# A windowed-attention and MLP kernel on one core: three more buffers in spent weights' space, a first copy in halves, last stores on two queues, and a new written-out order

## The chip, the core and the metric

The kernel runs on one core of a Trainium2 chip. TensorE (PE) multiplies, VectorE (DVE), ScalarE (ACT) and GpSimd (POOL) do the rest, and SyncE (SP) issues most of the DMAs. The metric is the device time of one execution in microseconds; the median of three runs stands for the kernel.

## The reference, cut to what matters

```python
x = layernorm(A_x)                                    # 2048 x 512
q, k, v = split(x @ wqkv)                             # 32 heads of 16
logits[s, w] = q[s] . k[s - 2*w] / 4,  w = 0..7       # masked where s - 2*w < 0
s = (softmax(logits) applied to v[s - 2*w]) @ wo
h  = gelu(layernorm(x) @ w1); four channel groups of h moved by -1, +1, -2, +2 positions
x1 = x + moved(h) @ w2
g  = silu(x1 + gelu(layernorm(x1) @ w3) @ w4)         # w3: 512 x 1376
out = x + s * g
```

All tensors are bf16. The mixer uses x normalized once, the MLP normalizes it once more.

## The kernel before, in words

The 2048 rows are worked in 4 chunks of 512, a chunk in 4 tiles of 128 rows. There is no planner at run time and no loop: a string `ORDER` (line 16) lists all steps by hand, and the last lines of the kernel call them one after the other. A token such as `w1.6.4` is step `w1` for tile 6 in PSUM bank 4. Each engine runs its own instructions in the order in which they stand in the list, and waits by semaphore for what another engine must have done; so where a token stands fixes what it queues behind.

The steps that matter here, with their engine and line:

- **Front.** `ldxp` and `ldxc` load x (SP). `st`, `nm0`, `nmv` take statistics and normalize (DVE). For chunk 0 PE transposes the normalized tile (`tr0`, line 353) and ACT copies it out of PSUM into `xnT` (`ev0a`, line 357); later chunks are transposed by DMA (`xT`).
- **Products of x, four matmuls of 512 columns a step.** `v` (line 460), `w1` (485) and `qk` (432) on PE; ACT takes the results away (`ev`, `eh`, `eqk`), `sv` stores v to DRAM from POOL's queue (`vt` has 3 buffers), `hTr` transposes h into `hT` by DMA (504), and `w2` (600) reads `hT`; `xa` (607, DVE) adds its result to x.
- **Attention.** `pw` (DVE, 519) multiplies q with shifted k, eight times a chunk. `lg` (PE, line 532) sums each head: two of the eight at once, 32 matmuls of 128 columns, in weight tiles of 128 x 32. `smx`, `ex`, `sms`, `smn` are the softmax (DVE, ACT) in one `E_c` buffer, and `tE` (587) transposes it into `att` by DMA. `vl` (699) loads shifted rows of v from DRAM as two halves of 512 KB into a value buffer `vs`, `vp` (705, DVE) multiplies them with `att`, and `ws` (718, PE, weight tiles of 128 x 32 again) sums over the window. Each `ws` of a chunk reads all four value buffers of the chunk. `oTr` (737) transposes the result by DMA, `wo` (757) is the last product, `sg` (764) multiplies with the gate.
- **MLP.** `x1Tr` (644) transposes, `w3` (657) and `eg` (666) make 11 pieces of h3 a chunk, `w4` (674) is 11 matmuls a tile, `ya` (681) adds, `si` (685) takes silu.
- **End.** Tiles 0 to 11 are added onto a copy of x in the output by DMAs with addition (`pre`, `soa`). Tiles 12 to 15 are finished on chip: `oTp` and `eoT` transpose on PE and ACT, `wo` for tiles 12 to 14, `woh` (782) in two halves of 256 columns for tile 15, then `ge`, `gb`, `fav` and `sgh`, `favh` (ACT and DVE) and the stores `so` and `soh`.

A rotating buffer is chosen when the program is built. `tags` (129) gives each use the buffer that was used longest ago, and can add buffers from a given use on. The value buffers are four of their own, from use 8 on also the space of `wqk_sb` (weights of `qk`), from use 12 on that of `hT`. `att` is a single buffer. PSUM has six banks for the products and one area of two for `lg`.

The loads of SP's queue are issued in their order; one that waits holds those behind it.

Of the kernel before, what the change touches and what calls it, by code (L numbers as in the profile page):

```python
# [16 lines left out]
ldxp.s.0 c_warm c_small ldv.s.0 kh.0 warmup.10.512.0 sqw ldv.s.1 c_ident ldxp.s.1 ldw1.s.0
c_elog st.0 st.1 sq0.0 nm0.0 sq0.1 rp.0 nm0.1 tr0.0.0 warmup.8.128.1 ev0a.0 tr0.1.2 v.0.0 rs.0
st.2 ev0a.1 ldw1.s.1 ldxp.s.2 st.3 c_sel sq0.2 v.1.2 ldxp.s.3 ev.0 rr.0 ldqk.s.0 nm0.2 sq0.3
ldqk.s.1 ev.1 c_zero nm0.3 tr0.2.0 w1.1.1 rp.1 ev0a.2 ldxc.s.2 ldwo.s.2 st.5 v.2.0 eh.1 st.4  # L20
w1.2.2 rs.1 st.6 tr0.3.3 sv.0 w1.0.4 ev0a.3 st.7 ldw2.s sv.1 ev.2 qk.0.0.3 rr.1 rp.2 eh.2 sv.2
rp.3 qk.0.2.0 eh.0 rs.2 eqk.0.0 v.3.2 hTr.0 rs.3 nmv.4 eqk.0.2 nmv.5 qk.0.7.3 rr.2 nmv.6 xT.2
ev.3 qk.0.6.0 st.11 eqk.0.7 sv.3 st.8 qk.0.5.2 eqk.0.6 rr.3 w1.3.3 nmv.7 eqk.0.5 st.10 qk.0.3.0
ldxc.s.3 eh.3 st.9 xT.3 qk.0.4.2 eqk.0.3 rp.5 rp.4 qk.0.1.3 rs.4 eqk.0.4 vl.s.0.0 kh.1 eqk.0.1
nb.4 vl.s.0.1 w1.4.2 rr.4 nm.9 rs.5 pw.0.0 vl.s.1.0 v.4.3 nm.8 v.5.0 pw.0.2 ev.4 eh.4 vl.s.3.1
w1.5.4 sv.4 pw.0.1 ev.5 xT.4 qk.1.2.2 eh.5 sv.5 pw.0.3 qk.1.5.0 eqk.1.2 rr.5 qk.1.7.4 eqk.1.5
st.15 ldwo.s.3 hTr.1 qk.1.4.2 st.12 eqk.1.7 lg.0.1 nb.5 eqk.1.4 st.13 v.6.4 nm.11 pw.0.6 nm.10
lg.0.0 v.7.2 ev.6 pw.0.7 sv.6 w1.6.4 vl.s.1.1 ev.7 pw.0.4 xT.5 lg.0.3 sv.7 pw.0.5 w1.7.2 hTr.2
v.8.0 st.14 lg.0.2 rp.6 rp.7 eh.7 w2.1.3 rs.7 smx.0 eh.6 ev.8 rs.6 v.9.2 hTr.3 w2.0.0 sv.8 ev.9
w1.9.4 sv.9 vl.s.2.0 nb.6 xa.1 ex.0 vl.s.2.1 qk.2.3.2 rr.7 st3s.1 qk.2.0.3 rr.6 xa.0 qk.2.6.1  # L30
eqk.2.0 nb.7 sms.0 eh.9 w2.4.0 qk.2.1.3 v.11.5 eqk.2.6 xa.4 nm.14 v.10.1 smn.0 nm.15 w2.3.0
ldw3.s.1 ev.10 st3s.0 tE.0 nm.12 w2.2.4 sv.10 xa.3 nm.13 qk.2.2.1 rq.0 xa.2 r3.0 ev.11 qk.2.7.0
st3s.3 eqk.2.2 sv.11 eqk.2.3 st3s.2 qk.2.5.5 vl.s.3.0 eqk.2.7 nm3.0 eqk.2.1 qk.2.4.2 rq.1 nm3.1
eqk.2.5 r3.1 st3s.4 w1.11.3 x1Tr.0 eqk.2.4 nm3.2 w1.8.5 vp.0 eh.11 w1.10.2 eh.8 w2.5.3 hTr.4
eh.10 vp.2 qk.1.6.5 hTr.5 qk.1.3.2 eqk.1.6 qk.1.1.0 kh.2 eqk.1.3 xa.5 vp.3 qk.1.0.5 eqk.1.1
w2.7.3 eqk.1.0 xT.7 w2.6.0 pw.1.3 xT.6 w2.8.5 pw.1.2 w2.9.2 v.14.1 xa.6 xa.7 lg.1.1 ev.14 st3s.6
v.13.3 ldw3.s.0 sv.14 pw.1.7 w1.13.1 pre.s.1 ev.13 pw.1.0 w1.12.0 sv.13 eh.13 w1.14.3 pw.1.1
eh.12 w1.15.1 hTr.6 eh.14 pw.1.4 lg.1.0 eh.15 v.12.3 ldw4.s.0 pw.1.6 hTr.7 ev.12 pw.1.5 qk.3.5.1
qk.3.2.0 sv.12 vp.1 eqk.3.5 kh.3 qk.3.6.3 eqk.3.2 qk.3.7.1 eqk.3.6 w2.11.0 eqk.3.7 pw.2.0 lg.1.2
xa.11 ws.1.1 ws.2.3 pw.2.2 eo.1 ws.0.0 eo.2 ws.3.4 eo.0 pw.2.1 w2.12.1 vl.s.4.1 eo.3 qk.3.1.0  # L40
oTr.1 nm3.3 xa.12 qk.3.4.4 eqk.3.1 xa.8 x1Tr.1 xa.9 qk.3.0.1 eqk.3.4 st3s.8 qk.3.3.2 eqk.3.0
st3s.9 w2.10.4 eqk.3.3 vl.s.8.0 st3s.7 vl.s.6.1 w2.15.1 xa.10 ldw4.s.1 w3.0.2.2 rq.3 rq.4
ldw4.s.2 xa.15 r3.3 vl.s.7.0 pw.3.0 w3.0.3.4 eg.0.2 r3.4 vl.s.6.0 w3.0.0.1 oTr.0 eg.0.3 nm3.7
nm3.6 w3.0.8.2 st3s.5 eg.0.0 x1Tr.3 w3.0.10.4 st3s.10 eg.0.8 st3s.11 w3.0.5.1 eg.0.10 rq.2
w3.0.4.2 st3s.15 r3.2 eg.0.5 rq.5 w3.0.1.4 st3s.12 r3.5 eg.0.4 nm3.5 w3.0.6.1 eg.0.1 nm3.4
lg.1.3 eg.0.6 w3.0.9.4 pw.2.3 pre.s.0 w3.0.7.1 eg.0.9 smx.1 vl.s.8.1 w2.14.2 vl.s.5.1 eg.0.7
x1Tr.2 w2.13.4 w4.0.1 xa.14 ex.1 xa.13 vl.s.7.1 st3s.14 st3s.13 w4.3.4 ya.0 rq.7 sms.1 si.0 r3.7
w4.1.1 ya.3 smn.1 si.3 w4.2.4 ya.1 nm3.10 si.1 nm3.11 ldwo.s.1 nm3.8 x1Tr.5 w3.1.1.1 nm3.9 ya.2
w3.1.3.2 rq.6 pw.2.4 si.2 tE.1 r3.6 eg.1.1 w3.1.9.4 w3.1.0.5 vl.s.5.0 nm3.14 x1Tr.4 w3.1.7.0
nm3.15 eg.1.0 eg.1.9 w3.1.5.1 vp.6 eg.1.7 eg.1.3 w3.1.6.4 eg.1.5 w3.1.8.2 eg.1.6 vp.7 w3.1.2.1  # L50
eg.1.8 w3.1.4.4 eg.1.2 w3.1.10.2 eg.1.4 vp.5 w3.2.0.1 eg.1.10 v.15.4 eg.2.0 nm3.13 vl.s.4.0
w4.5.2 ev.15 nm3.12 x1Tr.6 sv.15 x1Tr.7 w4.4.4 ya.5 si.5 vp.4 w4.7.2 vl.s.12.0 ya.4 si.4 lg.2.0
ya.7 ws.5.4 pw.2.6 si.7 lg.2.1 ws.6.2 eo.5 ws.7.1 pw.3.1 eo.6 w4.6.4 eo.7 pw.2.5 pw.2.7 lg.2.2
ws.4.1 ya.6 lg.2.3 pw.3.3 si.6 w3.2.9.4 eo.4 pw.3.5 w3.2.2.2 eg.2.9 w3.2.4.1 smx.2 w3.2.3.0
eg.2.4 eg.2.2 ldwo.s.0 w3.2.7.4 eg.2.3 pre.s.2 pw.3.2 w3.2.5.2 ex.2 w3.2.1.0 pw.3.4 wo.0.1
vl.s.13.0 eg.2.7 w3.2.6.5 sms.2 lg.3.0 lg.3.1 vl.s.12.1 eg.2.6 lg.3.2 eg.2.5 vl.s.13.1 w3.2.10.4
sg.0 eg.2.1 vl.s.11.0 smn.2 w3.2.8.2 soa.0 eg.2.10 wo.1.0 eg.2.8 pw.3.6 tE.2 wo.2.4 sg.1 oTr.2
w4.8.2 pw.3.7 soa.1 sg.2 soa.2 w4.10.4 ya.8 vl.s.9.1 si.8 vl.s.9.0 vp.8 vl.s.10.0 wo.3.2 wo.5.0
oTr.3 w3.3.0.1 sg.3 vl.s.10.1 sg.5 wo.4.5 soa.3 eg.3.0 ya.10 soa.5 lg.3.3 sg.4 w4.11.4 vl.s.11.1
smx.3 soa.4 si.10 w4.9.1 vp.9 ex.3 wo.6.5 ya.11 sms.3 si.11 w3.3.2.4 w3.3.10.0 eg.3.2 w3.3.5.2  # L60
sg.6 w3.3.8.3 smn.3 soa.6 w3.3.3.5 eg.3.5 eg.3.10 vp.10 w3.3.7.2 eg.3.3 eg.3.8 w3.3.9.0 eg.3.7
w3.3.4.3 vp.11 eg.3.9 w3.3.6.2 eg.3.4 w3.3.1.0 eg.3.6 ya.9 tE.3 ws.8.3 eg.3.1 ws.9.2 si.9
ws.11.0 ws.10.1 w4.12.5 vl.s.14.0 eo.10 eo.11 vp.13 eo.8 vl.s.14.1 eo.9 w4.13.3 vl.s.15.0
vl.s.15.1 ya.12 oTr.4 vp.12 si.12 w4.15.5 ya.13 vp.14 si.13 w4.14.3 ya.15 wo.7.2 vp.15 si.15
wo.8.5 oTr.5 wo.9.0 ya.14 ws.12.1 sg.8 si.14 ws.13.3 ws.14.4 sg.7 eo.12 soa.8 ws.15.5 eo.13 sg.9
soa.7 oTp.12.2 eo.15 wo.11.1 soa.9 eo.14 eoT.12 oTp.13.5 sg.11 wo.10.4 eoT.13 soa.11 oTp.15.1
sg.10 oTp.14.5 eoT.15 wo.13.2 eoT.14 soa.10 wo.12.1 ge.13 wo.14.5 gb.13 ge.12 fav.13 woh.15.0.2
gb.12 so.s.13 ge.14 woh.15.1.1 fav.12 sgh.15.0 so.s.12 gb.14 favh.15.0 sgh.15.1 soh.s.15.0
fav.14 favh.15.1 so.s.14 soh.s.15.1
# [4 lines left out]
def kernel(  # L74
# [280 lines left out]
    @step  # L355
    def ev0a(i):
        nc.scalar.activation(xnT_tile(0)[:, i, :, :], tr_t.pop(i), AF.Copy)
# [502 lines left out]
```

## Time and profile before

| | |
|---|---|
| median of 3 runs | 193.5 us (193.16 to 193.62) |
| the profiled execution's own time | 192.78 us |
| its span, first to last instruction | 191.0 us |
| PE busy | 97% of the span, 1430 matmuls |
| DVE, ACT, POOL busy | 86%, 63%, 22% |
| granted TensorE clock | 1.0 |
| moved by DMA | 39.25 MB, mean 205 GB/s |

The span is what the profile's rows add up to; the execution's own time is 1.8 us longer, and the median of the runs is 0.7 us above the profiled execution. A row of the timeline gives the start, the time taken, engine, line, operation and tiles, and how many instructions it merges. The end of a matmul is modelled and overlaps the next one, so that PE's pace is read from start to start: sixteen matmuls of 512 columns between two starts of the timeline take 3.45 us, four of them 0.86 us.

### The profile page before, as it was taken

How to read it: one execution, taken by the hardware profiler on the slowest of the kernel's cores; microseconds unless marked ns; L12 is line 12 of the kernel's file. 1: busy time of each engine (PE TensorE's matmuls, PEld its weight loads, DVE VectorE, ACT ScalarE, POOL GpSimd, SP SyncE). 2: the span in 40 equal slices, each digit the busy share in tenths (PEclk: the TensorE clock that was granted, in tenths of full speed). 3: DMA queues.
4: the chain of work that ended last, by engine and by line, in shares of the span. 5: the costliest groups of instructions: out<-in, count | busy, mean ns of one | idle time of the engine just before them, and what ended most of it. 6: DMA issues, size and time to landing. Idle time of an engine off the chain costs nothing.

```text
span 191.0 us, 3682 instructions
## 1 busy us (share of the span) xinstructions
PE 184.7 (97%) x1430; PEld 86.2 (45%) x1430; DVE 163.8 (86%) x270; ACT 120.8 (63%) x190; POOL 42.2 (22%) x70
## 2 busy tenths in 40 slices
...
GB/s 185 330 328 281 202 293 282 266 276 263 228 141 116 293 165 128 220 304 324 217 308 137 195 139 137 250 6 317 123 135 239 278 232 27 55 270 224 64 127 114
DMA packets 47841, 39.25 MB, mean 205 GB/s; under 512 B 35250, under 2 KB 41888, under 8 KB 47776
## 3 DMA queue, kind: packets, MB, share of 16 engines
...
q0 software_dynamic: 2528, 3.69, 10.0%
...
## 4 chain that ended last, share of the span: by engine, by line
PE 77%; DMA 12%; DVE 4%; SPq 2%; ACT 2%; issue 1%; DVEq 0%; ACTq 0%
PE mm L657 20%; PE mm L674 15%; PE mm L432 13%; PE mm L600 7%; PE mm L485 6%; PE mm L757 5%; PE mm L460 4%; DMA oT<-o 4%; DMA hT<-ht 4%; PE lg L532 3%; PE mm L718 3%; DMA xc<-in_A_x_dram 2%; DMA att<-E_c 2%; SPq L267 1%; DVE vs L705 1%; DVE st L330 1%
## 5 line engine op out<-in xcount | busy, mean ns | idle before, releaser
L657 PE MATMUL mm<-x1T,w_sb 128*128 128x512 bf16 (+1 forms) x176 | 39.3, 379 | 0.1
L705 DVE TENSOR_TENSOR vs<-vs,att 128x4096 bf16<-128x4096 bf16 x16 | 36.2, 2286 | 3.5 <-DMA att<-E_c 2.5
L674 PE MATMUL mm<-w_sb,h 128*128 128x512 bf16 (+1 forms) x176 | 39.1, 379 | 0.0
L519 DVE TENSOR_TENSOR pw<-qT,kT 128x2048 bf16<-128x2048 bf16 x32 | 37.6, 1219 | 1.4 <-PE lg L532 1.4
L666 ACT ACTIVATE h<-mm 128x512 bf16<-128x512 f32 (+1 forms) x44 | 24.7, 599 | 8.8 <-PE mm L657 8.5
L432 PE MATMUL mm<-xnT,wqk_sb 128*128 128x512 bf16 x128 | 29.3, 379 | 0.0
L674 PEld LDWEIGHTS <-h 128*128 128x128 bf16 (+1 forms) x176 | 16.9, 98 | 21.1 <-issue 0.8
L657 PEld LDWEIGHTS <-w_sb 128*128 128x128 bf16 (+1 forms) x176 | 17.3, 100 | 20.3 <-issue 0.5
L685 ACT ACTIVATE xr<-xr 128x512 bf16<-128x512 bf16 x16 | 10.1, 630 | 24.7 <-DVE xr L681 24.6
L820 POOL DMA_DIRECT2D out_dram<-xr x12 | 10.5, 945 | 58.0 <-DVE xr L764 57.7
L432 PEld LDWEIGHTS <-wqk_sb 128*128 128x128 bf16 x128 | 12.5, 98 | 15.1
...
L460 PE MATMUL mm<-wv_sb,xnT 128*128 128x512 bf16 x64 | 16.0, 380 | 0.0
L600 PE MATMUL mm<-w_sb,hT 128*128 128x512 bf16 x64 | 15.6, 379 | 0.1
L485 PE MATMUL mm<-w_sb,xnT 128*128 128x512 bf16 x64 | 15.6, 379 | 0.0
L681 DVE TENSOR_TENSOR xr<-mm,xr 128x512 bf16<-128x512 f32 x16 | 10.9, 681 | 4.7 <-PE mm L674 4.5
L757 PE MATMUL mm<-wo_sb,oT 128*128 128x512 bf16 x60 | 14.6, 379 | 0.2 <-DMA oT<-o 0.2
L470 ACT ACTIVATE vt<-mm 128x512 bf16<-128x512 f32 x16 | 9.5, 594 | 7.5 <-PE mm L460 6.1
L624 POOL TENSOR_TENSOR rstd<-nmr,mhalf 128x2 f32<-128x2 f32 x8 | 8.0, 998 | 28.0 <-DVE nmr L617 28.0
L496 ACT ACTIVATE ht<-mm,rs 128x512 bf16<-128x512 f32 x16 | 10.8, 688 | 4.9 <-DMA hT<-ht 3.2
L330 DVE BATCH_NORM_STATS2 st<-xc 128x6 f32<-128x512 bf16 x16 | 10.8, 674 | 2.9 <-DMA xc<-in_A_x_dram 2.9
L441 ACT ACTIVATE kT<-mm 128x512 bf16<-128x512 f32 x16 | 9.6, 599 | 4.4 <-PE mm L432 3.4
...
## 6 DMA issues: line engine op xcount, KB each, us to landing
vs<-v_dram SPq DMA_DIRECT2D x32, 512.0 KB, 6.2
v_dram<-vt POOLq DMA_DIRECT2D x16, 128.0 KB, 4.6
out_dram<-in_A_x_dram SPq DMA_DIRECT2D x3, 512.0 KB, 4.8
out_dram<-xr POOLq DMA_DIRECT2D x12, 128.0 KB, 3.9
...
xc<-in_A_x_dram SPq DMA_DIRECT2D x4, 256.0 KB, 4.9
wqk_sb<-in_A_wqkv_dram SPq DMA_DIRECT2D x2, 512.0 KB, 6.8
```

Source lines behind the costliest of these rows:

```text
L330: nc.vector.bn_stats(out=st1[:, i, :], in_=xtile(i))
L432: nc.tensor.matmul(pt, lhsT=wqk_sb[:, dt, nt * P : (nt + 1) * P], rhs=xnT[c][:, :, dt, :], start=(dt == 0), stop=(dt == ND - 1),)
L460: nc.tensor.matmul(pt, lhsT=xnT[c][:, jj, dt, :], rhs=wv_sb[:, dt, :], start=(dt == 0), stop=(dt == ND - 1),)
L485: nc.tensor.matmul(pt, lhsT=xnT[c][:, jj, dt, :], rhs=w1_sb[:, dt, :], start=(dt == 0), stop=(dt == ND - 1),)
L519: nc.vector.tensor_tensor(out=pw_t[c, u], in0=q_t[c], in1=k_t[c][:, :, DIL * u : DIL * u + CH], op=ALU.mult)
L600: nc.tensor.matmul(pt, lhsT=hT[:, plane, g, p0 : p0 + P], rhs=w2_sb[:, g, :], start=(g == 0), stop=(g == ND - 1),)
L657: nc.tensor.matmul(pt[:fs, :], lhsT=w3_sb[:, dt, ft * P : ft * P + fs], rhs=x1T[c][:, :, dt, :], start=(dt == 0), stop=(dt == ND - 1),)
L666: nc.scalar.activation(h3[c, ft][:fs, :], mm.pop(("w3", c, ft))[:fs, :], AF.Gelu_apprx_tanh)
L674: nc.tensor.matmul(pt, lhsT=h3[c, ft][:fs, jj * P : (jj + 1) * P], rhs=w4_sb[:fs, ft, :], start=(ft == 0), stop=(ft == NF - 1),)
L681: nc.vector.tensor_tensor(out=xr[i], in0=mm.pop(("w4", i)), in1=xr[i], op=ALU.add)
L705: nc.vector.tensor_tensor(out=vv, in0=vv, in1=att[c][:, :, H * jj : H * jj + H].unsqueeze(2).to_broadcast([P, NB * 2, DH, H]), op=ALU.mult,)
L757: nc.tensor.matmul(pt, lhsT=oT[i // 2][:, i % 2, dt, :], rhs=wo_sb[:, dt, :], start=(dt == 0), stop=(dt == ND - 1),)
```

## The change

The code, in full but for the order:

```diff
-    vs_tag = tags([f"vs{k}" for k in range(NVS)], {2 * TPC: ["wqk_sb"], 3 * TPC: ["hT"]})
+    vs_tag = tags([f"vs{k}" for k in range(NVS)], {8: ["wqk_sb"], 9: ["hT"], 10: ["w2v_sb"]})
+
+    att_tag = tags(["att"], {1: ["w1_sb"]})
...
-    wv_sb = fixed("wv_sb", [P, ND, D])
+    w2v_sb = fixed("w2v_sb", [P, 2, ND, D])
+    w2_sb = w2v_sb[:, 0, :, :]
+    wv_sb = w2v_sb[:, 1, :, :]
     w1_sb = fixed("w1_sb", [P, ND, D])
-    w2_sb = fixed("w2_sb", [P, ND, D])
...
     @step
+    def ev0h(i, h):
+        nc.scalar.activation(
+            xnT_tile(0)[:, i, 2 * h : 2 * h + 2, :], tr_t[i][:, 2 * h : 2 * h + 2, :], AF.Copy
+        )
+        if h:
+            del tr_t[i]
...
     def tE(c):
-        att[c] = rot("att", c, 1, [P, NB * 2, P])
+        att[c] = sb.tile([P, NB * 2, P], BF16, name="att", tag=att_tag[c])
```

So `att` alternates between its own buffer and the space of the `w1` weights, and the value buffers of chunk 2 (uses 8 to 10) lie in the space of the weights of `qk`, in `hT`, and in that of the weights of `w2` and `v` together; use 11 takes the buffer of use 4, and uses 12 to 15 those of 5 to 8. A step `fag` (an addition on POOL) is defined too and not used.

The order: the same steps, with three replaced. `ev0a.0` and `ev0a.1` become `ev0h.0.0 ev0h.0.1 ev0h.1.0 ev0h.1.1`; `so.s.12` becomes `so.a.12` and `soh.s.15.1` becomes `soh.a.15.1`, that is, they are issued from ACT's queue. All else is moved, and many PSUM banks are others. The places that the prediction speaks of (cut to PE's steps where only they matter):

```diff
-tr0.0.0 warmup.8.128.1 tr0.1.2 v.0.0 v.1.2 tr0.2.0 w1.1.1
+tr0.0.0 warmup.8.128.1 tr0.1.2 v.0.1 v.1.2 w1.0.0 tr0.2.1 w1.1.2
...
 # every group of lg and ws on PE, with the step before and after it
-qk.1.4 lg.0.1 v.6 lg.0.0 v.7 w1.6 lg.0.3 w1.7 v.8 lg.0.2 w2.1
+w2.1 lg.0.0 lg.0.1 w2.0 ... qk.2.0 lg.0.3 lg.0.2 w2.4
...
-v.14 lg.1.1 v.13 ... w1.15 lg.1.0 v.12 ... w2.11 lg.1.2 ws.1 ws.2 ws.0 ws.3 w2.12 ... w3.0.6 lg.1.3 w3.0.9
+w3.0.10 lg.1.1 lg.1.0 w2.8 ... w2.14 lg.1.2 lg.1.3 w2.12
...
-w4.7 lg.2.0 ws.5 lg.2.1 ws.6 ws.7 w4.6 lg.2.2 ws.4 lg.2.3 w3.2.9 ... w3.2.6 lg.3.0 lg.3.1 lg.3.2 w3.2.10 ... wo.4 lg.3.3 w4.11
+w3.1.4 lg.2.1 lg.2.0 qk.3.6 ... w3.1.2 lg.2.2 ws.2 ws.1 ws.0 ws.3 lg.2.3 w4.6 ... w3.3.0 lg.3.0 lg.3.2 ws.4 ws.5 lg.3.1 ws.7 ws.6 lg.3.3 w4.9
...
-w3.3.1 ws.8 ws.9 ws.11 ws.10 w4.12 ... wo.9 ws.12 ws.13 ws.14 ws.15 oTp.12
+wo.7 ws.10 ws.9 ws.11 ws.8 w4.13 ... w4.14 ws.13 ws.15 ws.12 ws.14 wo.8
```

```diff
 # SP's queue: the first value loads and the transposes of h near them
-hTr.0 xT.2 ldxc.s.3 xT.3 vl.s.0.0 vl.s.0.1 vl.s.1.0 vl.s.3.1 xT.4 ldwo.s.3 hTr.1
+ldxc.s.2 xT.2 ldxc.s.3 xT.3 hTr.0 ldw2.s hTr.1 ldwo.s.0 hTr.2 xT.4 vl.s.1.1
 # SP's queue: the end
-tE.3 vl.s.14.0 vl.s.14.1 vl.s.15.0 vl.s.15.1 oTr.4 oTr.5 so.s.13 so.s.12 soh.s.15.0 so.s.14 soh.s.15.1
+tE.3 vl.s.14.1 vl.s.12.0 vl.s.14.0 vl.s.15.0 vl.s.15.1 oTr.5 oTr.4 so.s.13 so.s.14 soh.s.15.0
 # PE near the end
-w4.12.5 w4.13.3 w4.15.5 w4.14.3 wo.7.2 wo.8.5 wo.9.0 ws.12.1 ws.13.3 ws.14.4 ws.15.5
+w4.13.3 wo.5.4 w4.12.5 w4.15.1 w4.14.0 ws.13.4 ws.15.3 ws.12.1 ws.14.5 wo.8.0 wo.9.3 wo.10.1
 # DVE there
-ya.12 ya.13 vp.14 ya.15 vp.15
+vp.12 vp.14 ya.12 sg.5 sg.7 vp.15
 # DVE after the last wo
-gb.13 fav.13 gb.12 fav.12 sgh.15.0 gb.14 favh.15.0 sgh.15.1 fav.14 favh.15.1
+gb.13 fav.13 gb.14 fav.14 gb.12 sgh.15.0 fav.12 favh.15.0 sgh.15.1 favh.15.1
 # PE and DVE, chunk 0's softmax maximum
+lg.0.3 lg.0.2 w2.4.2 v.10.5 qk.2.4.0 w2.6.1 w2.7.3 w1.11.2
+smx.0 nm3.3 xa.4
 # PE, the last of w1 and the w2 that needs it
+w1.14.0 w3.0.0.2 w3.0.2.3 qk.2.6.0 w2.10.4 w2.11.1 w3.0.8.2 qk.3.1.4 w2.14.1
```

ACT's tables (one for gelu, one for exp, one for silu, one for the square root) are loaded anew where its order changes the function; the new order has 15 such loads, the old one 18.

More of the change, by code (lines that the diff above doesn't have):

```diff
@@ L16 @@
 ORDER = """
[L17 to L69, printed above, removed]
+ldxp.s.0 c_warm c_small warmup.10.512.0 sqw c_ident kh.0 ldv.s.0 ldv.s.1 ldxp.s.1 ldw1.s.0
@@ new lines @@
+ldw1.s.1 c_zero st.0 ldxp.s.2 ldxp.s.3 st.1 sq0.0 ldqk.s.0 ldqk.s.1 nm0.0 sq0.1 rp.0 nm0.1
+tr0.0.0 warmup.8.128.1 ev0h.0.0 ev0h.0.1 st.2 tr0.1.2 v.0.1 st.3 ev0h.1.0 ev0h.1.1 sq0.2 v.1.2
+ev.0 nm0.2 sq0.3 rp.1 w1.0.0 ev.1 nm0.3 rs.0 sv.0 st.5 tr0.2.1 ldxc.s.2 w1.1.2 ev0a.2 sv.1 rr.0
+st.4 tr0.3.3 rs.1 v.2.1 ev0a.3 st.7 rp.2 rs.2 w1.2.4 ev.2 st.6 eh.0 v.3.3 sv.2 rp.3 rr.1 w1.3.1
+nmv.4 nmv.5 ev.3 qk.0.1.5 xT.2 eh.1 sv.3 qk.0.0.3 rs.3 qk.0.3.2 eh.2 eh.3 eqk.0.1 c_elog
+qk.0.4.1 qk.0.5.5 nmv.6 nmv.7 st.11 ldxc.s.3 st.10 st.8 eqk.0.3 eqk.0.5 qk.0.2.2 eqk.0.0
@@ new lines @@
+qk.0.6.4 eqk.0.2 st.9 eqk.0.4 qk.0.7.3 eqk.0.6 eqk.0.7 pw.0.1 rp.5 st.15 st.13 rp.4 xT.3 hTr.0
+ldw2.s hTr.1 w1.4.1 v.5.4 ldwo.s.0 ev.5 w1.5.3 v.4.2 ev.4 qk.1.4.4 rs.4 sv.4 v.6.5 w1.7.2 rr.3
+rr.2 eh.4 pw.0.2 kh.1 ev.6 sv.5 rs.5 nb.4 pw.0.0 st.12 eqk.1.4 eh.5 w1.6.1 qk.1.1.4 qk.1.2.3
+v.7.5 hTr.2 nm.8 nm.9 w2.1.0 pw.0.3 nb.5 rp.6 eh.6 xT.4 vl.s.1.1 eh.7 st.14 rp.7 lg.0.0 rs.7
+eqk.1.2 lg.0.1 ev.7 pw.0.5 w2.0.5 rs.6 eqk.1.1 nm.11 nm.10 pw.0.4 sv.7 qk.1.5.4 sv.6 xT.5
+qk.1.6.3 xa.1 nb.7 qk.1.0.2 nb.6 st3s.1 eqk.1.6 hTr.3 rr.4 xa.0 ldw3.s.0 st3s.0 eqk.1.5 pw.0.6
@@ new lines @@
+nm.13 nm.12 nm.15 qk.1.7.0 qk.1.3.4 w2.2.5 w1.9.3 w1.8.1 eh.9 eh.8 xa.2 rr.7 hTr.4 rr.5 rq.0
+w1.10.5 pw.0.7 r3.0 v.8.3 eh.10 st3s.2 nm.14 w2.3.1 nm3.0 nm3.1 eqk.1.3 w2.5.5 ev.8 qk.2.0.4
+xa.3 st3s.3 eqk.1.7 eqk.1.0 xT.6 lg.0.3 rq.1 kh.2 xa.5 lg.0.2 r3.1 w2.4.2 smx.0 ldw3.s.1 sv.8
+xT.7 x1Tr.0 v.10.5 qk.2.4.0 w2.6.1 eqk.2.4 nm3.3 xa.4 ex.0 w2.7.3 w1.11.2 xa.6 st3s.6 nm3.2 xa.7
+qk.2.5.1 eqk.2.0 x1Tr.1 eh.11 ev.10 sv.10 rr.6 v.9.0 v.11.3 w1.13.4 eqk.2.5 ev.9 hTr.5 qk.2.7.2
+w1.15.1 eqk.2.7 w1.12.0 vl.s.2.0 vl.s.0.0 ldw4.s.2 qk.2.2.2 vl.s.3.1 eh.12 pw.1.0 st3s.4 st3s.7
```

38 lines of the change are left out of this document (added).

## The prediction

> **What bounds the kernel now.** I read the page's busy times first, then PE's waits, then the chain that ended last, then PE's timeline at the places which the chain names.
>
> ```profile
> span 191.0 us, 3682 instructions
> ...
> PE 184.7 (97%) x1430; PEld 86.2 (45%) x1430; DVE 163.8 (86%) x270; ACT 120.8 (63%) x190; POOL 42.2 (22%) x70
> ```
>
> PE is the bound. The change leaves the number and sizes of all matmuls alone, so what it can win is only what PE loses between them, plus the head before its first useful matmul and the tail after its last. The waits of PE's weight loads show the losses (line, releaser: us, times, longest):
>
> ```profile
> PEld L532 <- issue: 5.1, 12, 0.4
> ...
> PEld L718 <- issue: 0.8, 2, 0.4
> ...
> PEld L757 <- DMA oT<-o: 0.7, 1, 0.7
> PEld L600 <- DMA hT<-ht: 0.4, 1, 0.4
> ```
>
> Fourteen times the weight load stands still for 0.42 us with nothing to wait for: always at the first load of a run of `lg` (L532) or `ws` (L718). These are the steps with weight tiles of 128 x 32 among steps with tiles of 128 x 128. A part is hidden behind the last matmul; the chain (start, us) shows what PE pays:
>
> ```profile
> 61.44 0.86 PE mm L460 x4
> 62.30 0.59 PE lg L532 x32
> 62.90 0.97 PE mm L460 x4
> 63.87 3.45 PE mm L485 x16
> ...
> 122.71 0.45 PE lg L532 x32
> ```
>
> A step of four matmuls takes 0.86 us (3.45 for sixteen), and an `lg` step that stands between `ws` steps takes 0.45. From 61.44 to 63.87 are 2.43 us for work of 0.86 + 0.45 + 0.86 = 2.17: **one visit to the small tiles costs 0.26 us**, however many steps it holds.
>
> The other losses are real waits, read from start to start on PE:
>
> ```profile
> 7.07 1.90 PE L460 MATMUL mm<-wv_sb,xnT 128*128 128x512 bf16 x8
> 9.12 0.40 PE L353 MATMUL mm<-ident,xr 128*128 128x128 bf16 x4 [0.15 <-DVE xr L342]
> ...
> 35.68 1.27 PE L600 MATMUL mm<-w_sb,hT 128*128 128x512 bf16 x4
> 36.90 1.02 PE L460 MATMUL mm<-wv_sb,xnT 128*128 128x512 bf16 x4
> 37.97 1.02 PE L600 MATMUL mm<-w_sb,hT 128*128 128x512 bf16 x4
> ...
> 79.78 1.89 PE L600 MATMUL mm<-w_sb,hT 128*128 128x512 bf16 x8
> 81.73 1.45 PE L657 MATMUL mm<-x1T,w_sb 128*128 128x512 bf16 x6
> ...
> 175.41 1.03 PE L757 MATMUL mm<-wo_sb,oT 128*128 128x512 bf16 x4
> 176.64 1.90 PE L757 MATMUL mm<-wo_sb,oT 128*128 128x512 bf16 x8 [0.20 <-DMA oT<-o]
> ...
> 185.53 1.04 PE L782 MATMUL mm<-wo_sb,oT 128*128 128x256 bf16 x8
> ```
>
> Eight matmuls (1.73) fill 7.07 to 9.12: 0.32 lost before `tr0.2`, which waits for `nm0.2`. `w2.1` takes 35.68 to 36.90, 0.36 too much; the next step 0.21 too much; `w2.15` and its neighbour 79.78 to 81.73, 0.22 too much; `wo.7` 175.41 to 176.64, 0.37 too much. Together 1.16 us in the middle, 0.32 at the head. PE ends at 186.57, so the tail is 4.4 us.
>
> **The change part by part.**
>
> *Fewer visits.* In the old order PE goes to the small tiles 14 times, in the new one 9 times (the change lists them): `lg` steps stand in pairs, and with `ws`. 5 x 0.26 = **-1.3 us**. Nothing covers this, since PE never rests; and PE has no other work that could hide it.
>
> *The waits of the middle.* What stands before the late transposes, in the chain and in SP's queue:
>
> ```profile
> 28.23 7.85 DMA hT<-ht
> ...
> 168.66 7.93 DMA oT<-o
> ```
>
> ```profile
> 21.71 2.55 SPq L699 DMA_DIRECT2D vs<-v_dram  x4
> ...
> 165.97 2.45 SPq L699 DMA_DIRECT2D vs<-v_dram  x4
> ```
>
> Both transposes were issued some 3 to 7 us behind four value loads of 512 KB, and took 7.9 us. In the new order no value load stands before `hTr.0` to `hTr.2`, and 19 steps of PE lie between `w1.3`, the last that `hTr.1` needs, and `w2.1`. Before the last `oTr` stand two loads in place of four, and `wo.8` comes 12 us of PE's work after the `ws` that feeds it. The added buffers allow that: only `vl.15` is still to be loaded there. `x1T`'s wait at 81.7 goes too, as `w3.0.6` stands well behind its transposes. I take all of it: **-1.16**. The second `att` ends a wait of DVE, not of PE (2.5 us in L705's row below); it counts only through `oT`, which is in this sum.
>
> *The head.*
>
> ```profile
> L357 ACT ACTIVATE xnT<-mm 128x512 bf16<-128x512 bf16 x4 | 2.4, 597 | 1.3 <-PE mm L353 1.3
> ```
>
> ```profile
> 2.67 0.95 SPq L238 DMA_DIRECT2D w_sb<-in_B_w_dram  x2
> ```
>
> ```profile
> w_sb<-in_B_w_dram SPq DMA_DIRECT2D x2, 256.0 KB, 4.9
> ```
>
> `w1.0` moves between `v.1` and `tr0.2`: PE works from 8.8 to 9.67 in place of waiting until 9.12. Its weights were issued by 3.15 and land by about 8.1, in time. The copies in halves are not in the trace: a half costs between nothing and a full 0.6 us, so the pair adds up to 1.2 us on ACT ahead of `sq0.2`, or starts `v.0` up to 0.06 us sooner (the gap behind `tr0.1`). I take 0.4 us a half; `sq0.2` is then some 0.3 us later and `tr0.2` ready at about 9.4, hidden by `w1.0`; at 0.6 us, `v.1`'s second half would start 0.1 late. **-0.32**, ends -0.4 and -0.2.
>
> *The tail.*
>
> ```profile
> 188.37 0.38 SPq L802 DMA_DIRECT2D out_dram<-xr  x1
> ```
>
> ```profile
> out_dram<-xr SPq DMA_DIRECT2D x2, 64.0 KB, 1.6
> ...
> out_dram<-xr POOLq DMA_DIRECT2D x12, 128.0 KB, 3.9
> ```
>
> DVE has the same ten steps behind the last `wo`; `gb.12` now precedes `sgh.15.0` and waits for ACT's copy, some 0.15 us later. The last store no longer queues behind `so.s.14` on SP, worth 0.2 us (it was issued at 188.37, DVE was done at 188.12). Sum nothing. What ACT's queue takes to land a store is not in the trace: from SP's 1.6 to POOL's 3.9 us. I take SP's, the other plain store of this size, and keep +2.3 for the range. The Trainium skill ("DMA: Bandwidth & Descriptors", Issuing engines are not separate DMA queues) says that DMAs of all issuing engines run on the same 16 DMA engines, so that several issuers save the issue time alone. By that rule the second queue gains no more than the 0.38 us of one issue, and the sum would stay; the trace of before, whose plain stores all go from SP, cannot show it.
>
> *Nothing elsewhere.* Three table loads fewer are 3.8 us of ACT, which is 63% busy; the moved weights buffers cost no instruction.
>
> *New waits.* I laid the new order's steps along PE at these durations and followed DVE's, ACT's and SP's orders beside them. Three inputs come close:
>
> ```profile
> L705 DVE TENSOR_TENSOR vs<-vs,att 128x4096 bf16<-128x4096 bf16 x16 | 36.2, 2286 | 3.5 <-DMA att<-E_c 2.5 <-DMA vs<-v_dram 0.6 <-issue 0.4
> ...
> L681 DVE TENSOR_TENSOR xr<-mm,xr 128x512 bf16<-128x512 f32 x16 | 10.9, 681 | 4.7 <-PE mm L674 4.5
> ...
> L764 DVE TENSOR_TENSOR xr<-mm,xr 128x512 bf16<-128x512 f32 x12 | 8.0, 678 | 2.4 <-PE mm L757 2.4
> ...
> L550 DVE TENSOR_TENSOR lg<-lg,mx 128x1024 f32<-128x1024 f32 x4 | 4.9, 1232 | 0.1
> L547 DVE TENSOR_REDUCE mx<-lg 128x128 f32<-128x1024 f32 x4 | 4.9, 1222 | 0.0
> ```
>
> ```profile
> vs<-v_dram SPq DMA_DIRECT2D x32, 512.0 KB, 6.2
> ...
> hT<-ht SPq DMA_TRANSPOSE x8, 4.2
> ```
>
> (a) Behind `lg.0.2` DVE runs `smx.0` (1.22 + 1.23 and its masks), `nm3.3`, `xa.4`, some 4.1 us, while PE has five steps, 4.3 us, until `w1.11` needs the bank of `xa.4`: no margin. (b) At the end DVE runs `ya.12`, `sg.5`, `sg.7`, `vp.15`: 0.68 x 3 + 2.29 = 4.3 us less overlap, against `w4.15` and `w4.14`, 4.8 us: 0.5. (c) `hTr.7` must land within the seven steps (6.0 us) from `w1.14` to `w2.14`: after ACT's gelu and 4.2 us 0.9 are left. I put **+0.3** for such places, a quarter of what the old order lost.
>
> Sum: -1.3 - 1.16 - 0.32 + 0.3 = -2.5 us against the profiled execution, 191.0 to 188.5 in its span; carried to the median, 193.5 - 2.5 = **191.0**. Bare of new waits it would be 190.7, with a us of them 191.7.
>
> **The rivals.**
>
> *The waits come back elsewhere.* The new order may lose on banks and buffers as much as the old one, 1.2 to 2 us. For it: DVE at 86% with margins of 0 to 0.5 us. Against: I find few close places. Only the visits and the head remain: 193.5 - 1.3 - 0.3 = 191.9, at 2 us 192.7.
>
> *`hTr.7` lands late.* It is the one transpose with a margin under a us. At 7.85 us, as in the chain above, it would cost 7.85 - 4.2 - 0.9 = 2.7 us, and the gain is gone: 190.7 + 2.7 = 193.4, no change. Against: only `ldwo.s.3` and one transpose stand near it in SP's queue.
>
> *The last value buffer, slower.* `vl.15` takes the buffer of use 8, free only when all four `ws` of chunk 2 are done; from there to `ws.13` PE has four `w4` and a `wo`, 10.4 us, and DVE needs 2.3 for `vp.15`. So its second half must land within 7.2 us of its issue (median 6.2); each us more is a us of PE. It decides the sign from 7.2 + 2.8 + 0.6 = 10.6 us on. The slowest transfers above took 7.9, for a loss of 0.7; 11.5 us would give 195.0.
>
> **How the numbers follow.** About 0.6 us, 0.3%, is what a measurement can tell from no change. Forecast (190.2 to 191.7): 0.62. Waits elsewhere (191.7 to 192.9): 0.20. `hTr.7` or a slow store on ACT's queue (+2.3), 192.9 to 194.1: 0.10. The last buffer, or a wait of its size: 0.08. The range 190.2 to 192.9 leaves out the last two. Faster 0.82, same 0.10, slower 0.08.
>
> **What would show it.** PE's weight loads with 9 stops of 0.4 us and not 14; no wait of PE for `hT` or `oT`; `tr0.2` without a gap; PE's end near 184 us and the tail still 4.4. Wrong it would be if `w1.11`, `w2.14` or `ws.13` start late, or if the last store lands later than 1.6 us after its issue.

## The result, and the profile after

The changed kernel takes 190.52 us (median of 6 runs, 189.73 to 190.75), the kernel before 192.88 us beside it (6 runs, 192.36 to 193.62): a ratio of 0.987, 95% interval 0.983 to 0.990. The profiled execution took 190.75 us, its span went from 191.0 to 189.0. Forecast were 191.0 us, and 188.5 for the span.

The first rows of the page and PE's waits in the changed kernel (line, releaser: us, times, longest; lines have moved by up to 15, `lg` is L543 now, `ws` L729):

```profile
span 189.0 us, 3685 instructions
...
PE 182.8 (97%) x1430; PEld 87.0 (46%) x1430; DVE 165.1 (87%) x270; ACT 112.8 (60%) x189; POOL 42.7 (23%) x70
```

```profile
PEld L543 <- issue: 2.9, 7, 0.4
...
PEld L356 <- DVE xr L345: 1.9, 2, 1.1
...
PEld L729 <- issue: 0.4, 1, 0.4
PEld L768 <- issue: 0.4, 1, 0.4
PEld L685 <- issue: 0.4, 1, 0.4
PEld L729 <- DVE xr L775: 0.4, 1, 0.4
PEld L496 <- issue: 0.3, 1, 0.3
```

The stops of 0.4 at the small tiles are 7 + 1 + 1 = 9, as the order says (at the ninth DVE is named, for the same 0.4). `wo` (L768) and `w4` (L685) pay one each on the way back from `ws`. No row names `hT` or `oT` any more. What is left, beside the warm-up matmuls (L321), is L356, the first transposes, which wait for DVE, 0.3 at `w1` (L496) and 0.2 at `v` (L471).

What a visit costs in the new order stands in the chain of the changed kernel, where a pair of `lg` steps goes in at once:

```profile
31.53 0.86 PE mm L611 x4
32.39 1.05 PE lg L543 x64
33.44 0.97 PE mm L611 x4
34.41 4.32 PE mm L443 x20
...
51.11 0.02 issue
51.13 1.02 PE mm L496 x4
52.15 0.86 PE mm L443 x4
```

From 31.53 to 34.41 are 2.88 us; the work is 0.86 + 2 x 0.45 + 0.86 = 2.62. So the visit costs 0.26 with two steps as it did with one. The last three rows show the one new wait of the middle: `w1.11` at 51.13 takes 0.02 + 1.02 where four matmuls need 0.86, **0.18 us**, for the bank of `xa.4`.

Near the end, PE's timeline of the changed kernel (start, us):

```profile
164.24 2.55 PE L685 MATMUL mm<-w_sb,h 128*128 128x512 bf16 x11
166.63 1.03 PE L768 MATMUL mm<-wo_sb,oT 128*128 128x512 bf16 x4
167.50 7.30 PE L685 MATMUL mm<-w_sb,h 128*128 128x512 bf16 x33
174.72 1.48 PE L729 MATMUL mm<-vs,sel 128*32 128x512 bf16 x24
...
183.51 1.04 PE L793 MATMUL mm<-wo_sb,oT 128*128 128x256 bf16 x8
```

Forty-eight matmuls of 512 columns fill 164.24 to 174.72: 48 x 0.216 = 10.4 of 10.5 us. `ws.13` at 174.72 starts with no loss but the visit's; the last value buffer and DVE were in time. The last row is PE's last work.

The stores of the end, issue on each queue and then the time from issue to landing (median of the group):

```profile
185.47 0.37 ACTq L839 DMA_DIRECT2D out_dram<-xr  x1
185.70 0.33 SPq L813 DMA_DIRECT2D out_dram<-xr  x1
186.37 0.34 ACTq L813 DMA_DIRECT2D out_dram<-xr  x1
```

```profile
out_dram<-xr ACTq DMA_DIRECT2D x1, 128.0 KB, 1.9
...
out_dram<-xr SPq DMA_DIRECT2D x1, 64.0 KB, 1.9
out_dram<-xr ACTq DMA_DIRECT2D x1, 64.0 KB, 1.6
```

The last store, from ACT's queue, lands 1.6 us after its issue, as the last store did before, from SP's queue. PE's last work ends at 184.55 (183.51 + 1.04), 2.02 earlier than before; from there to the end of the span are 4.4 us, as before.

The one place that went the other way is the head. PE's timeline of the changed kernel (in brackets the idle time and its releaser), and the chain of the changed kernel there:

```profile
3.72 1.91 PE L321 MATMUL mm<-warm 128*128 128x512 bf16 x4
...
6.83 0.39 PE L356 MATMUL mm<-ident,xr 128*128 128x128 bf16 x4
...
8.83 1.03 PE L496 MATMUL mm<-w_sb,xnT 128*128 128x512 bf16 x4
10.11 0.40 PE L356 MATMUL mm<-ident,xr 128*128 128x128 bf16 x4 [0.26 <-DVE xr L345]
```

```profile
2.15 5.68 DMA xc<-in_A_x_dram
...
7.85 0.71 DVE st L333
```

`w1.0` fills 8.83 to 9.69 as meant, and `tr0.2` still waits 0.42, to 10.11. The chain says why: the second half of x's first chunk, issued at 2.15, took 5.68 us and landed at 7.83. In the kernel before the same load was issued at 2.17 and landed at 6.77:

```profile
2.17 4.61 DMA xc<-in_A_x_dram
```

So the two executions compare like this: from `tr0.2` on, 9.12 to 186.57 before and 10.11 to 184.55 after, 177.45 and 174.44 us, 3.01 less; 0.86 of it is `w1.0`, which now stands ahead of `tr0.2`. The rest won 2.15 us, and the head lost 0.13: from 9.12 to 10.11 - 0.86 = 9.25. What had to be found out was whether this late load is the change's doing, and which part of the change carries the 2.15.

### The profile page after: what moved, and what is told of

Its sections match the earlier page's. It is cut to its first block, busy times and chain, and to the rows that moved or that the text cites. A ratio compares the mean times of both kernels' runs of the same rounds, so it can differ in the third digit from the quotient of the medians.

```text
span 189.0 us, 3685 instructions
## 1 busy us (share of the span) xinstructions
PE 182.8 (97%) x1430; PEld 87.0 (46%) x1430; DVE 165.1 (87%) x270; ACT 112.8 (60%) x189; POOL 42.7 (23%) x70
## 4 chain that ended last, share of the span: by engine, by line
PE 85%; DMA 4%; DVE 4%; issue 2%; POOL 2%; SPq 1%; ACT 1%; POOLq 0%
PE mm L668 20%; PE mm L685 18%; PE mm L443 15%; PE mm L611 8%; PE mm L496 7%; PE mm L471 6%; PE lg L543 4%; PE mm L768 4%; DMA xc<-in_A_x_dram 3%; PE mm L729 3%; POOL out_dram L835 2%; DMA out_dram<-xr 1%; DVE st L333 1%; DVE xr L775 1%; DVE xr L786 1%
## 5 line engine op out<-in xcount | busy, mean ns | idle before, releaser
L530 DVE TENSOR_TENSOR pw<-qT,kT 128x2048 bf16<-128x2048 bf16 x32 | 38.3, 1214 | 3.4 <-PE lg L543 2.4
L668 PE MATMUL mm<-x1T,w_sb 128*128 128x512 bf16 (+1 forms) x176 | 40.9, 379 | 0.0
L685 PE MATMUL mm<-w_sb,h 128*128 128x512 bf16 (+1 forms) x176 | 39.4, 379 | 0.0
L677 ACT ACTIVATE h<-mm 128x512 bf16<-128x512 f32 (+1 forms) x44 | 23.9, 602 | 23.3 <-PE mm L668 17.6
L443 PE MATMUL mm<-xnT,wqk_sb 128*128 128x512 bf16 x128 | 30.6, 379 | 0.0
L835 POOL DMA_DIRECT2D out_dram<-xr x12 | 11.0, 1117 | 74.0 <-DVE xr L775 74.0
L685 PEld LDWEIGHTS <-h 128*128 128x128 bf16 (+1 forms) x176 | 16.9, 98 | 20.8 <-issue 0.4
L489 POOL DMA_DIRECT2D v_dram<-vt x16 | 9.6, 601 | 30.6 <-ACT vt L481 27.2
L471 PE MATMUL mm<-w2v_sb,xnT 128*128 128x512 bf16 x64 | 15.8, 379 | 0.0
L496 PE MATMUL mm<-w_sb,xnT 128*128 128x512 bf16 x64 | 15.8, 379 | 0.0
L611 PE MATMUL mm<-w2v_sb,hT 128*128 128x512 bf16 x64 | 15.7, 380 | 0.0
L768 PE MATMUL mm<-wo_sb,oT 128*128 128x512 bf16 x60 | 14.3, 379 | 0.0
L452 ACT ACTIVATE qT<-mm 128x512 bf16<-128x512 f32 x16 | 9.4, 605 | 7.8 <-PE mm L443 7.7
L635 POOL TENSOR_TENSOR rstd<-nmr,mhalf 128x2 f32<-128x2 f32 x8 | 9.1, 1136 | 19.8 <-DVE nmr L628 19.7
```

Source lines behind the costliest of these rows:

```text
L443: nc.tensor.matmul(pt, lhsT=wqk_sb[:, dt, nt * P : (nt + 1) * P], rhs=xnT[c][:, :, dt, :], start=(dt == 0), stop=(dt == ND - 1),)
L452: nc.scalar.activation(dst.rearrange("p (n i) -> p n i", i=TPC), mm.pop(("qk", c, nt)).rearrange("p (i n) -> p n i", i=TPC), AF.Copy,)
L471: nc.tensor.matmul(pt, lhsT=xnT[c][:, jj, dt, :], rhs=wv_sb[:, dt, :], start=(dt == 0), stop=(dt == ND - 1),)
L496: nc.tensor.matmul(pt, lhsT=xnT[c][:, jj, dt, :], rhs=w1_sb[:, dt, :], start=(dt == 0), stop=(dt == ND - 1),)
L530: nc.vector.tensor_tensor(out=pw_t[c, u], in0=q_t[c], in1=k_t[c][:, :, DIL * u : DIL * u + CH], op=ALU.mult)
L611: nc.tensor.matmul(pt, lhsT=hT[:, plane, g, p0 : p0 + P], rhs=w2_sb[:, g, :], start=(g == 0), stop=(g == ND - 1),)
```

## The experiments

Twelve kernels in three groups; a group ran on one chip, beside runs of the kernel before. Ratios are to the kernel before of the same group.

| kernel | median us | ratio, 95% interval |
|---|---|---|
| before (first group) | 193.04 | |
| e1_after | 190.30 | 0.984, 0.980 to 0.988 |
| e2_zero_late | 189.87 | 0.983, 0.979 to 0.987 |
| e3_split5 | 191.21 | 0.989, 0.986 to 0.993 |
| e4_before_zero_early | 193.44 | 1.000, 0.997 to 1.003 |
| before (second group) | 193.02 | |
| e5_old_order_new_buffers | 192.75 | 1.000, 0.997 to 1.003 |
| e6_before_vl_late | 193.38 | 1.003, 1.001 to 1.006 |
| e7_one_att | 191.66 | 0.994, 0.992 to 0.996 |
| f1_best | 189.85 | 0.985, 0.982 to 0.988 |
| before (third group) | 192.67 | |
| g1_after_again | 190.09 | 0.988, 0.984 to 0.991 |
| g2_sp_stores | 190.10 | 0.986, 0.983 to 0.990 |
| g3_whole_copies | 189.99 | 0.987, 0.983 to 0.990 |
| g4_best_again | 190.07 | 0.986, 0.983 to 0.990 |

### The late load of the head: e1, e2, e4

My first theory was that POOL's zeroing DMA (`c_zero`), which is issued at 1.50 in the changed kernel and at 7.13 before, gets in front of x's loads. The rival was that the landing varies from execution to execution.

`e1_after` is the changed kernel as it is.

> The changed kernel once more, beside three others on the same chip. Both theories of the head: it has the new order as it stands. Theory (the small DMA that zeroes the rows ahead of v, now issued at 1.5 us in place of 7.1, holds up the loads of x): the second half of x's first chunk lands near 7.8 us again and tr0.2 starts near 10.1. Rival (the late landing was chance of one execution): it lands near 6.8, tr0.2 starts near 9.7. Time 2.0 to 2.8 us below the kernel before.

`e2_zero_late`:

```diff
-ldw1.s.1 c_zero st.0
+ldw1.s.1 st.0
...
-ev.1 nm0.3
+ev.1 c_zero nm0.3
```

> The changed kernel with the zeroing DMA put back behind ev.1, as in the old order; nothing else is moved. Theory: the second half of x lands near 6.8 us (1.0 earlier than in the unchanged new order), tr0.2 starts at 9.7 without a wait, PE ends 0.4 to 0.5 us earlier, and the time is 0.4 to 0.5 us lower than that of the unchanged new order. Rival (chance, or the half copies): nothing changes, within 0.2 us.

`e4_before_zero_early` is the kernel before, with `c_zero` right behind `c_ident`.

> The kernel before with one step moved: the zeroing DMA ahead of the constants of lg, right behind the identity. Theory: the loads of x from the second half of chunk 0 on land 0.9 to 1.1 us later, tr0.2 starts near 10.1 in place of 9.1, and the kernel is 0.7 to 1.0 us slower than before. Rival (chance): same as before.

e2 did not do what it was meant to do: nothing stands ahead of `c_zero` on POOL at either place, so it was issued at 1.51 again, and the kernel is e1's order of instructions on every engine. That made it a second look at the same order, and it told more than it was built for. e1 and e2 differ in their heads by 0.6 us all the same. PE's timeline of e1, then of e2:

```profile
3.71 1.91 PE L321 MATMUL mm<-warm 128*128 128x512 bf16 x4
...
7.01 0.43 PE L356 MATMUL mm<-ident,xr 128*128 128x128 bf16 x4
...
9.91 0.39 PE L356 MATMUL mm<-ident,xr 128*128 128x128 bf16 x4
```

```profile
3.71 1.16 PE L321 MATMUL mm<-warm 128*128 128x512 bf16 x4
...
6.46 0.39 PE L356 MATMUL mm<-ident,xr 128*128 128x128 bf16 x4
...
9.32 0.39 PE L356 MATMUL mm<-ident,xr 128*128 128x128 bf16 x4
```

In neither does `tr0.2` wait: it starts 2.90 and 2.86 us behind `tr0.1`, which is about what the work between them takes. x's load landed at 7.06 in e1 and at 6.77 in e2. In e4 the zeroing DMA was issued at 1.50, as in the changed kernel, and x's load landed at 6.75, as in the kernel before. Over all fourteen traces of this document the load lands at 6.96 on the mean of the nine with the zeroing DMA at 1.50, and at 6.89 on the mean of the five with it at 6.5 or later. The theory falls; the rival stands.

### What a visit costs: e3

```diff
 # the changed kernel, five pairs of lg pulled apart, on PE
-lg.0.0 lg.0.1 w2.0
+lg.0.0 w2.0 lg.0.1
-qk.2.0 lg.0.3 lg.0.2
+lg.0.3 qk.2.0 lg.0.2
-w3.0.10 lg.1.1 lg.1.0
+lg.1.1 w3.0.10 lg.1.0
-w2.14 lg.1.2 lg.1.3
+lg.1.2 w2.14 lg.1.3
-w3.1.4 lg.2.1 lg.2.0
+lg.2.1 w3.1.4 lg.2.0
```

> The changed kernel with five of its pairs of lg steps pulled apart on PE by one other step, so that PE goes to the small weight tiles 14 times in place of 9; no step is later for another engine by more than 0.6 us. Theory (0.26 us of PE for each visit): 1.2 to 1.3 us slower than the unchanged new order, weight loads standing still 14 times. Rival (the stop is hidden behind the last matmul, and the gain came from the waits): within 0.3 us.

The weight loads of e3 show the old number of stops:

```profile
PEld L543 <- issue: 5.1, 12, 0.4
```

The median is 0.9 us above e1's and 1.3 above e2's, of one group and one chip. From the start of `tr0.2` to the start of its last step PE takes 175.10 us in e3, 173.75 in e1 and 173.76 in e2: 1.35 for five visits, 0.27 each. PE's other waits are those of the changed kernel, so the price of a visit is shown by itself.

### Order or buffers: e5 and e6

e5 is the new code (the second `att`, value buffers 8 to 10 in spent weights) with the order of before, its copies and its stores.

> The new buffers (second att, value buffers 8 to 10 in spent weights' space) with the old order, old copies and old stores. Theory A, the gain lies in the order: the buffers alone leave the 14 visits of PE to the small weight tiles, hT's wait at w2.1 (0.36) and the late w2.15; they can only let tE.3 go without waiting for vp.11, bring vl.14 and vl.15 earlier and so take wo.7's wait for oT (0.37): 0 to -0.5 us against the kernel before, ratio 0.997 to 1.000. Theory B, the buffers carry the gain and the order only follows them: -1.2 us or more, ratio below 0.994.

The buffers alone gain nothing that can be measured (interval 0.997 to 1.003). The one wait which they were to take away is gone: `vl.14`'s two loads had landed when `oTr.4` was issued, so that it had two loads ahead of it and not four; it landed in 3.5 us and not 7.9, and `wo.8` started on time. That wait isn't in every execution, though. e4 has the old buffers and differs from the kernel before in the head alone; there `oTr.4` took 7.4 us, and `wo.7` to `wo.9` (twelve matmuls, of which the profile has eleven) lose nothing but the 0.09 that PE loses ahead of any visit:

```profile
175.60 2.75 PE L757 MATMUL mm<-wo_sb,oT 128*128 128x512 bf16 x11
178.28 1.91 PE L718 MATMUL mm<-vs,sel 128*32 128x512 bf16 x32
```

PE's waits of e5 show that the visits and the wait for `hT` stay:

```profile
PEld L543 <- issue: 5.1, 12, 0.4
...
PEld L611 <- DMA hT<-ht: 1.1, 1, 1.1
...
PEld L729 <- issue: 0.8, 2, 0.4
```

The 14 stops are there, and `w2.1` loses 1.15 us to `hT` and not 0.36; in e4 it loses 0.59, so a part of this is the scatter between executions. The chain of e5 at that place:

```profile
26.64 3.33 SPq L270
...
30.01 7.24 DMA hT<-ht
...
37.30 0.82 PE mm L611 x3
```

SP takes 3.33 us to issue the load of `wo`'s weights just ahead of `hTr.1` (2.36 before, 2.83 in e4); then the transpose takes 7.24, behind the four value loads.

e6 takes one of those edits by itself, in the kernel before:

```diff
-xT.3 vl.s.0.0 vl.s.0.1 vl.s.1.0 vl.s.3.1 xT.4 ldwo.s.3 hTr.1 vl.s.1.1 xT.5 hTr.2 hTr.3
+xT.3 xT.4 ldwo.s.3 hTr.1 vl.s.1.1 xT.5 hTr.2 hTr.3 vl.s.0.0 vl.s.0.1 vl.s.1.0 vl.s.3.1
```

> The kernel before, with only its first four value loads (512 KB each) moved on SP's queue from ahead of hTr.1 to behind hTr.3. Theory A (the value loads are what makes the transpose of h take 7.9 us): hTr.1 lands 3 to 5 us after its issue, w2.1's 0.36 and the next step's 0.2 go, -0.4 to -0.6 us, ratio 0.997 to 0.998. Theory B: hTr.1 takes as long without them, or vp.0 now waits for its value load and the wait comes back on PE: within 0.2 us of before.

Theory A is right on the transpose: `hTr.1` was issued at 25.77 and landed 4.36 us later, and `w2.1` and the step behind it run at full pace. On the time it is wrong: the kernel is not faster but 0.3% slower. Theory B has the wait come back on PE, and it does, though not through the value load that B named. The rows of PE's timeline in e6, at `w2.1` and a third of the way down the kernel, and one of DVE's between them:

```profile
35.61 1.04 PE L600 MATMUL mm<-w_sb,hT 128*128 128x512 bf16 x4
36.49 1.03 PE L460 MATMUL mm<-wv_sb,xnT 128*128 128x512 bf16 x4
...
61.85 0.66 PE L532 MATMUL lg<-pw,e_log 128*32 128x128 bf16 x32
63.05 1.02 PE L460 MATMUL mm<-wv_sb,xnT 128*128 128x512 bf16 x4 [0.53 <-DVE xr L607]
```

```profile
52.23 4.49 DVE L705 TENSOR_TENSOR vs<-vs,att 128x4096 bf16<-128x4096 bf16 x2 [0.79 <-DMA att<-E_c]
```

Six value loads now go out in one row, from 36.88 to 40.25, and the transpose of the softmax behind them, `tE.0`, took 6.08 us (3.75 before). So `vp.0`, which reads `att`, waits 0.79 us for it and starts at 52.23 (51.69 before); `vp.2`, `vp.3`, `xa.6` and `xa.7` behind it on DVE start as much later, and `v.13` at 63.05 loses 0.60 us more than before, waiting for the bank of one of these `xa`. That undoes the 0.55 won at `w2.1` and the step behind it: the wait was not removed but passed on, from `hT` through `att` and DVE to PSUM. From `tr0.2` on e6 takes 0.65 us longer than the kernel before; the rest (0.25 at the second product behind `tr0.2`, 0.29 more at `wo.8` for `oT`) can't be put down to the edit by one trace. In the changed kernel `vp.0` starts at 89.45 (51.69 before), long after those `xa`, so that a late load has nothing to hold there.

### The second att: e7

e7 is the changed kernel with one `att` buffer, and `tE.1`, `tE.2`, `tE.3` each behind the last `vp` that reads `att` of the chunk before:

```diff
-    att_tag = tags(["att"], {1: ["w1_sb"]})
+    att_tag = tags(["att"], {})
```

> The changed kernel with a single att buffer, and each tE behind the last vp that reads att of the chunk before (tE.1 behind vp.2, tE.2 behind vp.7, tE.3 behind vp.8 on SP's queue, their natural places with one buffer); all else as changed. Theory A: the second att is needed by the new order, since vp.8 is the last reader of att of chunk 2 and stands late: tE.3 lands some 3 us later, vp.13 waits for it, ws.13 starts 2 to 3 us late, +2 to +3 us against the changed kernel, span about 191 to 192. Theory B: DVE has slack there and the second att only removed a wait that cost PE nothing: within 0.3 us of the changed kernel.

Its median is 1.1 to 1.6 us above the changed kernel's three (190.52, 190.30, 190.09), so A in sign, smaller than forecast; f1 below, the one version of the changed kernel run in the same group, is 1.8 us lower than e7. PE's timeline of e7, beside the rows of the same place in the changed kernel above:

```profile
163.77 2.55 PE L685 MATMUL mm<-w_sb,h 128*128 128x512 bf16 x11
167.18 1.02 PE L768 MATMUL mm<-wo_sb,oT 128*128 128x512 bf16 x4 [0.86 <-DVE xr L775]
168.04 4.92 PE L685 MATMUL mm<-w_sb,h 128*128 128x512 bf16 x22
173.38 1.89 PE L685 MATMUL mm<-w_sb,h 128*128 128x512 bf16 x8 [0.42 <-DVE xr L775]
```

Eleven matmuls need 2.37 us and have 3.41 (163.77 to 167.18): 1.04 lost; the 22 behind them lose 0.59. The wait isn't at `ws.13`, where I had looked for it: DVE waited 2.4 us for `att` at `vp.13`, and the `sg` steps behind it on DVE came late, whose banks PE's `wo.5` and `w4` need. With the old order the second `att` and the new value buffers together brought nothing that the medians show (e5); with the new one, which puts other work behind those `vp`, the kernel without the second `att` keeps only about half of the gain. Buffers and order can't be priced apart.

### A better version, and the small parts: f1, g1 to g4

f1 is the changed kernel with two moves:

```diff
 # DVE
-nm3.3 xa.4
+xa.4 nm3.3
 # POOL
-c_zero ... rs.0
+rs.0 c_zero
```

> The changed kernel with xa.4 ahead of nm3.3 on DVE, so that the PSUM bank of w1.11 is free 0.4 us earlier, and with the zeroing DMA of POOL behind rs.0, truly later (it was first on POOL in the two kernels that were to test it). Theory A: w1.11's wait of 0.18 us goes, and nothing else moves: -0.2 us against the changed kernel, PE's excess over the pace 3.0. Theory B: nm3.3 is now late for x1Tr.0 or w3 and the 0.18 comes back elsewhere: same as the changed kernel. For the loads of the head: if the zeroing DMA delays them, the second half of x's first chunk lands before 6.7 us and tr0.2 starts by 9.2; if their landing varies by itself, it lands somewhere in 6.7 to 7.9 again.

The chain of f1 at `w1.11`:

```profile
50.29 0.86 PE mm L496 x4
51.15 0.86 PE mm L443 x4
```

The 0.18 us are gone. The zeroing DMA was now issued at 6.62, and x's load landed at 7.02: in the scatter, so the theory of `c_zero` falls here too. f1's 189.85 stood alone in its group, so it was run again beside the changed kernel, with the two small edits of the change undone one at a time:

> The changed kernel as it is, beside the three others of this group. About 190.3 us, ratio 0.985. Its head: the second half of x's first chunk lands between 6.7 and 7.9 us, tr0.2 starts between 9.3 and 10.1; if the head gains what was forecast on the mean of executions (0.32), tr0.2's start less the 0.86 of w1.0 ahead of it lies near 8.8, against 9.1 in the old order.

> The changed kernel with the two stores of ACT's queue back on SP's (so.s.12 and soh.s.15.1, at the same places of the order). Theory A, the second queue saves issue time only, and the last store waits for DVE, not for SP: soh.s.15.0 is issued 0.1 later behind so.s.12, soh.s.15.1 when favh.15.1 is done, landing 1.6 later: 0 to +0.1 us, same. Theory B, the second queue was worth an issue of 0.35 us or more: the time from the end of PE to the end of the span grows from 4.6 to 5.0.

> The changed kernel with ev0a.0 and ev0a.1 in place of the four half copies. Theory A: v.0 starts 0.06 to 0.3 later behind tr0.1 (in the old order the gap was 0.05 longer), sq0.2 some 0.2 earlier; the start of tr0.2 as after, 0 to +0.2 us. Theory B: ACT's longer pair of copies is what makes nm0.2 late in the changed kernel, and without it tr0.2 never waits: -0.2 to -0.4 us.

> The version with xa.4 ahead of nm3.3 and the zeroing DMA behind rs.0 once more, now beside the changed kernel. Theory A: w1.11's 0.18 us is gone for good: -0.2 us against g1_after_again's median (-0.1 to -0.6 with the scatter of the head). Theory B: the difference was the scatter of the head alone: within 0.1 us.

The medians of all four lie within about 0.1 us (189.99 to 190.10). The stores on ACT's queue are worth nothing that shows: with both back on SP (g2) the time from the start of PE's last step to the end is 5.07 us, against 5.03 in g1. With whole copies (g3) `v.0` starts 0.18 us later behind `tr0.1` than its work needs, and `tr0.2` 3.01 us behind `tr0.1` and not 2.86; that 0.15 us of the head is all that the halves bring, too little for the medians to show. For f1's edit the traces agree, from the start of `tr0.2` to the start of PE's last step 173.61 us in f1 and in g4 against 173.75 in g1, but the times don't show these 0.14, and I can't call f1 faster than the changed kernel.

## Why the prediction was right, and where it was not

*Fewer visits, -1.3.* Right: nine stops, 0.26 us a visit in the new order, and 1.35 us back for five visits in e3.

*The waits of the middle, -1.16.* Right that all four are gone; the size is that of one execution. In e4, which has the old order but for one small DMA, the four places lose 0.59, 0.20, 0.22 and nothing, 1.01 in all. The reason given, loads ahead of transposes, is shown for `hT` by e6 (7.85 us with four loads ahead, 4.36 without). For `oT` (7.93, and 3.5 with two loads ahead in e5) it fits, but the number of loads alone doesn't set the time: two of the four ahead of `hT` had landed, too, when it was issued (at 25.57 and 28.01; the issue is at 28.23). Nothing was run for the 0.22 at `w2.15`. And the new order doesn't make every transpose fast, it gives PE other work: one of `oT`, issued at 148.44, takes 8.1 us in the changed kernel, and no step of PE waits for it. What the prediction left out is that the loads' new places are only free because DVE's order was rebuilt with them; e6 gives the gain at `hT` back.

*The second `att`.* The prediction counted it through `oT` alone, as it ends a wait of DVE and not of PE. That reading failed, though no term of the sum hangs on it: without it (e7) PE loses 1.04 and 0.59 us at places that have nothing to do with `oT`, because DVE frees two PSUM banks late.

*New waits, +0.3.* 0.18 us, at place (a), `w1.11`; (b) and (c) held. `hTr.7` landed 2.7 us after its issue and the second half of `vl.15` 5.3 us after its own, where 7.2 was the limit: none of the rivals came about.

*Visits, waits and new waits together.* They make -2.16, and the two profiled executions show 2.15 less. The agreement to 0.01 is luck: the new wait is 0.12 smaller than the +0.3, and against the six traces with the order of the changed kernel on PE the two traces with the old order that leave its loads alone (before and e4) give between 1.98 and 2.24.

*The head, -0.32.* In the compared executions this step failed: +0.13. The working took the landing of x's load as given (6.77 us), and it is not. Over the fourteen traces it lies between 6.22 and 7.83 us with issues within 0.02 us of each other. The step's mechanism holds: in the old order `tr0.2` starts 2.35 us behind that landing in three traces of four (in e6, at 6.22, PE's own work sets it); in the new order it starts at the later of landing + 2.28 and `tr0.1` + 2.86 (2.90 in e1, 3.01 in g3), with 0.86 us more work done. At the kernel before's landing and `tr0.1` (6.77 and 6.79) this gives 9.65 - 0.86 = 8.79 against 9.12: the -0.33 of the forecast. At 7.83 the old order would have started `tr0.2` at 10.18 and the new one did so at 10.11 with `w1.0` done, so the edit gained there too. Over the traces, `tr0.2`'s start less `w1.0` is 8.72 us on the mean of the ten with the new order (8.37 to 9.25), against 9.13 for the four with the old (8.80 to 9.51). So the mechanism was right, and a single execution's head is known to half a us at best. One thing stays open: the load itself lands at 7.02 on the mean of the ten and at 6.72 on that of the four, and with this scatter four traces can't tell whether the change has a part in these 0.3. The guess of 0.4 us for a half copy was near: the four halves take 1.33 us on ACT in g1, the two whole copies 1.27 in g3.

*The tail, 0.* Right: PE's end to the span's end is 4.4 us before and after, the ACT queue's store landed in 1.6 us, and putting it back on SP changes nothing (g2). The rule of the Trainium skill ("DMA: Bandwidth & Descriptors", Issuing engines are not separate DMA queues), that several issuers save issue time alone, agrees with this: here even that came to nothing, as the last store waits for DVE.

The whole, -2.5 forecast, is -2.4 by the medians of the first comparison and -2.6 to -2.7 by those of g1 and e1. The forecast of 191.0 lies 0.5 above the 190.52 measured since it started from 193.5, the median of three runs; six runs gave 192.88.
